# Mode weights in one load of 2 KB runs a tile, in place of two half-partition loads of 4 KB runs

## The chip, the cores and the metric

The kernel runs on one core of one Trainium2 chip. The core has TensorE (PE) for matrix products, VectorE (DVE), ScalarE (ACT), GpSimd (POOL) and SyncE (SP); the last two issue its DMAs, and sixteen DMA engines carry them. The metric is the device time of one execution in microseconds, as a median of several runs. A profiled execution gives the instruction and DMA records.

## The reference

Causal attention over 8 batches, 8 heads, 576 positions and 64 dimensions, with a bias from a running sum of `max(s, 0)`, is followed by a spectral mixing layer. The heads are laid side by side to `x` of shape (8, 576, 512). Cut to what matters here:

```python
X = np.fft.rfft(x, axis=1)                       # 64 modes are used
Xr, Xi = (np.real(X[:, :n_modes]), np.imag(X[:, :n_modes]))
Yr = einsum('bmd,mde->bme', Xr, w_r) - einsum('bmd,mde->bme', Xi, w_i)
Yi = einsum('bmd,mde->bme', Xr, w_i) + einsum('bmd,mde->bme', Xi, w_r)
y = np.fft.irfft(Y, n=S, axis=1)
u = x + y
return u + np.maximum(u @ w_ch, 0.0)
```

`w_r` and `w_i` are 64 x 512 x 512 in float32, 67 MB each. Every element is used once for each of the 8 batches, so nearly all bytes that the kernel reads are these weights.

## The kernel before

The attention runs over 32 steps `n`, each a pair of heads of one batch; 8 steps (the batches) make one of four groups `g`, and a group is a block of 128 channels. A step forms scores, exponentials and the products with `v`, which end in `x_all`. `fft(n)` then takes the 64 Fourier modes of this block by products with a table `Ff_sb` (L427) and copies them from PSUM to `xs` (L437).

`modes(g, c)` multiplies eight modes `8c` to `8c+7` of group `g` with their weights (L449): 16 products of a 32-column block of `xs` with 512 columns of weights, in four column groups of PE, added up in one PSUM tile. The 32 columns of a block belong to two modes, real and imaginary parts and 8 batches.

The weights are read in the order of `wq`: group, chunk `c`, real or imaginary `ri`, and `par`. A tile holds four modes by 128 channels by 512 columns in bfloat16, converted by the DMA from float32, and there are 128 tiles. In the kernel before, `loads_w` fills a tile by two transfers, each of 64 partitions: half `h` takes every second mode, and one partition of it holds two neighbouring channels of a mode, so that 4 KB are read in one run and 2 KB are written in one. The two halves of the partitions belong to different modes, so `xs` has a block for each half and parity of the channel (`q`), with zeros where a mode is not the half's own, and `Ff_np` has its columns sorted by `h`. `fft` therefore runs over two parities, five row blocks and two halves: 20 products of 96 columns and four copies.

The first 8 tiles of weights go to places not in use yet (`early`), the others to rings of 11 and 6 buffers. Which tiles are asked for in which step is planned ahead (`on_chip`, `used`), from how many earlier tiles are used up by then. `load` merges the lists of a step (q, k, v for three steps ahead, and weights) by their positions in them, and issues each transfer on POOL's queue (L224). POOL works through its queue in order; where a buffer is not free or too many transfers are out, it waits, and everything behind it waits too. `load` asks for a single packet request a transfer in both kernels:

```python
nc.gpsimd.dma_start(out=dst, in_=src, single_packet=True)
```

`wch_sb`, the matrix `w_ch`, is loaded once from POOL (L570). SP's queue carries the constants at the start, in each step two rows of the running sum to `qtA` and `qtB` (`cum_rows`, L318 and L319), at the end the row spreads to `yv` (`spread`, L484) and the stores of the result (L766).

After the last step, the eight chunks of the last group remain (from L773): `modes(3, c)`, a transposition and a product with `w_ch` for each, mixed with stored products of `x`. The last chunk's products are mixed with the first sums of the output (`meanwhile`), in another order than in the other calls. Then all pairs of output tiles are finished and stored.

Of the kernel before, what the change touches and what calls it, by code (L numbers as in the profile page):

```python
# [9 lines left out]
FP32 = mybir.dt.float32  # L10
FP16 = mybir.dt.float16
BF16 = mybir.dt.bfloat16
# [6 lines left out]
def kernel(  # L19
# [11 lines left out]
    nc = tc.nc  # L31
    B, H, S, D = q.shape
    NM = moe_w_r.shape[0]
    DM = H * D
    P = 128
    NT = (S + P - 1) // P
    tails = [min(P, S - T * P) for T in range(NT)]
# [8 lines left out]
    MC = 8  # L46
# [7 lines left out]
    W = 2 * P  # L54
    NWN = S // W
    NK = 2 * NWN
    HM = NM // 2
    HP = P // 2


    ident_np = np.eye(P, dtype=np.float32)
# [7 lines left out]
    m_idx = np.arange(NM, dtype=np.float64)  # L69
    ang = 2.0 * np.pi * np.outer(t_idx, m_idx) / S  # L70
    Ff_np = np.zeros((SP, 3 * NM), dtype=np.float16)
    for h in range(2):
        for i, f in enumerate((np.sin(ang), np.cos(ang), -np.sin(ang))):
            Ff_np[:S, (3 * h + i) * HM : (3 * h + i + 1) * HM] = f[:, h::2]
    cmv = np.where(m_idx == 0, 1.0, 2.0) / S
    G_np = np.zeros((NM, 2, SP), dtype=np.float64)
    G_np[:, 0, :S] = cmv[:, None] * np.cos(ang.T)
# [16 lines left out]
    gp = ctx.enter_context(tc.tile_pool(name="globals", bufs=1))  # L94


    x_all = gp.tile([P, NG, B, NT, P], FP16, name="x_all")
    y_acc = gp.tile([P, NCK, DM], FP32, name="y_acc")

    xs = [gp.tile([P, 2, 2, 2, 2, B, HM], BF16, name=f"xs{i}") for i in range(2)]  # L100
    xs_flat = [t.rearrange("p q k h r b m -> p (q k h r b m)") for t in xs]
    ident16h = gp.tile([P, P], FP16, name="ident16h")
    Ff_sb = gp.tile([P, NT, 3 * NM], FP16, name="Ff_sb")
    G_sb = gp.tile([P, SP], FP16, name="G_sb")
# [4 lines left out]
    auxpool = ctx.enter_context(tc.tile_pool(name="aux_psum", bufs=2, space=PSUM))  # L109
# [24 lines left out]
    p_sb = [ap_.tile([P, poff[-1]], FP16, name=f"p_sb{i}") for i in range(NP_)]  # L134
    p4 = [ap_.tile([P, P], FP16, name=f"p4_{i}") for i in range(2)]

    temp = xs_flat[1].bitcast(FP32)
    ident32, negm32, s_sb = temp[:, :P], temp[:, P : P + 2 * W + NL], temp[:NPAIR, -S:]
    ident16 = ap_.tile([P, P], BF16, name="ident16")
    negm = ap_.tile([P, 2 * W + NL], BF16, name="negm")  # L140
# [49 lines left out]
    wt = {}  # L190
# [3 lines left out]
    def ring_of(k):  # L194
        if k < NE:
            return None
        return int(k < LW2 and (k - NE) % (WA + WB) >= WA)

    def loads_w(upto):
        todo = []  # L200
        while len(wt) < min(upto, len(wq)):
            g, c, ri, par = key = wq[len(wt)]
            i = ring_of(len(wt))
            if i is None:
                t = early[len(wt)]
            else:
                t = (wpool, wpool2)[i].tile([P, WM, DM], BF16, name="w_sb", tag="w")
            src = (moe_w_r, moe_w_i)[ri]
            m0 = c * MC + par * MC // 2
            for h in range(2):  # L210
                todo.append((
                    t[HP * h : HP * h + HP].rearrange("p (m q) e -> p m (q e)", q=2),
                    src[m0 + h : m0 + MC // 2 : 2, g * P : (g + 1) * P, :].rearrange(
                        "m (p q) e -> p m (q e)", q=2
                    ),
                ))
            wt[key] = t
        return todo

    def load(*lists):  # L220

        todo = [((i + 0.5) / len(l), x) for l in lists for i, x in enumerate(l)]
        for _, (dst, src) in sorted(todo, key=lambda t: t[0]):
            nc.gpsimd.dma_start(out=dst, in_=src, single_packet=True)  # L224
# [10 lines left out]
    for n in range(N):  # L235
# [3 lines left out]
        while nt < min(w, len(wq)):  # L239
            i = ring_of(nt)  # L240
# [37 lines left out]
    with tc.tile_pool(name="cum_psum", bufs=1, space=PSUM) as cpsum:  # L278
# [5 lines left out]
            out=cum, data0=spos, data1=zer, initial=0.0, op0=ALU.add, op1=ALU.add  # L284
# [16 lines left out]
        for x in range(2):  # L301
            rows = slice(NL * x, NL * x + NL)
            nc.vector.tensor_copy(
                out=cumt4[rows, :], in_=cumt_sb[rows, NK, x::2]
# [8 lines left out]
    def cum_rows(n):  # L313
        if n >= N:
            return
        g, b = divmod(n, B)
        p0 = b * H + 2 * g
        nc.sync.dma_start(out=qtA[n % NQ][D : D + 1, :], in_=ncum_sb[p0 : p0 + 1, :])  # L318
        nc.sync.dma_start(out=qtB[n % NQ][0:1, :], in_=ncum_sb[p0 + 1 : p0 + 2, :])  # L319
# [98 lines left out]
    def fft(n):  # L418
        if n < 0:
            return  # L420
        g, b = divmod(n, B)
        ps = auxpool.tile([P, 2, 3 * HM], FP32, name="ft_ps", tag="aux")
        for q_ in range(2):
            for T in range(NT):
                nT = tails[T]
                for h in range(2):
                    nc.tensor.matmul(  # L427
                        ps[HP * h : HP * h + HP, q_, :],
                        x_all[:nT, g, b, T, q_::2],
                        Ff_sb[:nT, T, 3 * HM * h : 3 * HM * (h + 1)],  # L430
                        start=(T == 0), stop=(T == NT - 1),
                        tile_position=(0, HP * h), skip_group_check=True,
                    )
        for h in range(2):
            rows = slice(HP * h, HP * h + HP)
            for k in range(2):
                nc.vector.tensor_copy(  # L437
                    out=xs[g % 2][rows, :, k, h, :, b, :],
                    in_=ps[rows, :, k * HM : (k + 2) * HM].rearrange("p q (r m) -> p q r m", r=2),
                )  # L440

    def modes(g, c, meanwhile=None):


        ps = auxpool.tile([P, DM], FP32, name="yp", tag="aux")
        cols = xs[g % 2].rearrange("p q k h r b m -> p q k (h r b) m")

        def product(ri, q_, cg):
            nc.tensor.matmul(  # L449
                ps[32 * cg : 32 * cg + 32, :],  # L450
                cols[:, q_, 1 - ri, :, c * MC // 2 + cg],
                wt[(g, c, ri, cg // 2)][:, 2 * (cg % 2) + q_, :],
                start=(ri == 0 and q_ == 0), stop=(ri == 1 and q_ == 1),
                tile_position=(0, 32 * cg), skip_group_check=True,
            )

        for x in range(4):
            ri, y = divmod(x, 2)
            if meanwhile and x in meanwhile:
                meanwhile[x]()  # L460
            for z in range(4):
                if meanwhile:
                    product(ri, z // 2, 2 * y + z % 2)
                else:
                    product(ri, y, z)
        if g == 0:
            nc.vector.tensor_copy(out=y_acc[:, c, :], in_=ps)
        elif g < NG - 1:
            nc.vector.tensor_tensor(out=y_acc[:, c, :], in0=ps, in1=y_acc[:, c, :], op=ALU.add)
        else:  # L470
            yb = spool.tile([P, DM], FP16, name="y_sb", tag="y")
            for cols in halves if c == NCK - 1 else [slice(0, DM)]:
                nc.vector.tensor_tensor(
                    out=yb[:, cols], in0=ps[:, cols], in1=y_acc[:, c, cols], op=ALU.add
                )
            if c >= NCK - 2:
                spread(c, 0, yb)
            return yb
# [3 lines left out]
    def spread(c, which, rows):  # L482

        nc.sync.dma_start(out=yv[16 * c : 16 * c + 16, :, which, :], in_=rows)  # L484
# [53 lines left out]
    with tc.tile_pool(name="sc_psum", bufs=2, space=PSUM) as scpool, \  # L538
            tc.tile_pool(name="tr_psum", bufs=1, space=PSUM) as trpool, \
            tc.tile_pool(name="av_psum", bufs=1, space=PSUM) as avpool:  # L540
        cum_rows(0)
        transposes(0, 0)
        transposes(0, 1)
        load(loads_qkv(2))
        pad_p()
        for n in range(N):
            if n in (0, 2):
                nc.vector.memset(xs_flat[n // 2].bitcast(FP32), 0.0)
            tails_due = loads_tails(n // B + 1)[n % B - 3 : n % B - 2] if 2 < n % B < 5 else []
            load(loads_qkv(n + LA) + tails_due, loads_w(on_chip[n]))  # L550
            cum_rows(n + 1)
            scores(n, 0)
            av(n - 1, 1)
            transposes(n + 1, 0)
            scores(n, 1)
            i = first_pairs[n - N + len(first_pairs)] if n >= N - len(first_pairs) else None
            if i is not None:
                first_transposed(i, 0)
            transposes(n + 1, 1)
            fft(n - 1)  # L560
            av(n, 0)
            if i is not None:
                first_product(i, 0)
                first_transposed(i, 1)
            for c in mode_steps.get(n, []):
                modes(c // NCK, c % NCK)
            if i is not None:
                first_product(i, 1)
            if n == N // 2:
                nc.gpsimd.dma_start(out=wch_sb, in_=moe_w_ch.rearrange("(dt p) e -> p dt e", p=P))  # L570
        av(N - 1, 1)
        fft(N - 1)
    load(loads_w(len(wq)))
    at.close()

# [7 lines left out]
    zpool = ctx.enter_context(tc.tile_pool(name="z_psum", bufs=2, space=PSUM))  # L583

    NLOC = 4
    old = xs_flat[0]
    xt_sb = [
        old[:, i * 2 * DM : (i + 1) * 2 * DM].bitcast(FP16).rearrange("p (x t c) -> p x t c", x=2, c=P)
        for i in range(2)
# [199 lines left out]
    c = NCK - 2  # L789
# [21 lines left out]
    for x in range(2):  # L811
        dts = slice(x * DT // 2, (x + 1) * DT // 2)
        ps = auxpool.tile([P, DT // 2, P], FP16, name="yt_ps", tag="aux")
# [88 lines left out]
```

## Time and profile before

| | |
|---|---|
| median of 3 runs | 453.28 us (452.77 to 454.39) |
| profiled execution: time / span | 452.77 / 451.0 us |
| mean granted clock of PE | 0.879 |
| weight loads of POOL | 256 of 256 KB written (240 to `w_sb`, 16 to early places) |
| q, k, v loads | 32, 32, 72 |
| DMA in all | 93.83 MB, mean 208 GB/s |
| HBM read / written | 164.56 MB / 9.44 MB |

Durations in the profile are those of single instructions; matrix products are pipelined, so that neighbouring ones overlap. The page cuts the span in 40 equal slices of 11.3 us with one digit for the busy tenths. Sizes of DMA packets are those of the bytes written; a weight packet reads twice as many. A line like "L224 POOL" is a DMA's issue and descriptor work on POOL, and not its transfer; transfers are listed with their time from issue to landing. The chain is followed back from the last instruction to what released it.

### The profile page before, as it was taken

The numbers are of one execution on the slowest core, as the hardware profiler recorded it, in microseconds if no ns is written. First come the engines' busy times: TensorE is split into PE (matmuls) and PEld (weight loads), VectorE is DVE, ScalarE is ACT, GpSimd is POOL, SyncE is SP. The second block draws the span as 40 slices with busy tenths as digits, with TensorE's granted clock in tenths as the row PEclk, the third lists the DMA queues.
The fourth block names the chain that finished last, engine by engine and source line by source line (L and its number), as shares of the span: only waits on it lengthen the run. The fifth ranks groups of instructions, "written<-read, shape, count | busy, mean of one in ns | idle before, by whom it ended". The sixth has DMA issues, their size and how long they took to land.

```text
span 451.0 us, 11579 instructions
## 1 busy us (share of the span) xinstructions
PE 359.5 (80%) x4745; PEld 226.5 (50%) x4745; DVE 257.3 (57%) x599; ACT 222.1 (49%) x390; POOL 241.2 (53%) x397
## 2 busy tenths in 40 slices
PE   1789999997566989946777777698897858879995
PEld 1456666665334666624555445456564425534432
DVE  7774776774333576723446545456654643662796
ACT  1584778565333566733435443456550323331774
POOL 7766765765566676455675665566544444420000
PEclk9995999997665699966769989889996986999999
DMA  9999999999999999999999999999999999994688
GB/s 182 200 204 206 204 204 205 205 207 207 207 207 201 196 192 200 208 207 207 204 203 207 208 205 207 207 205 203 207 210 211 209 209 209 210 218 91 236 299 316
DMA packets 77796, 93.83 MB, mean 208 GB/s; under 512 B 30432, under 2 KB 40160, under 8 KB 77744
## 3 DMA queue, kind: packets, MB, share of 16 engines
q0 software_dynamic: 68240, 81.81, 104.8%
q1 hardware_dynamic: 9504, 11.29, 7.9%
q8 instruction: 37, 0.61, 0.5%
q14 instruction: 15, 0.12, 0.1%
HBM read 164.56 MB, written 9.44 MB: 386 GB/s over the span
## 4 chain that ended last, share of the span: by engine, by line
DMA 48%; PE 33%; DVE 9%; issue 5%; POOL 2%; ACT 2%; SPq 0%; DVEq 0%; POOLq 0%; ACTq 0%
DMA w_sb<-in_moe_w_i_dram 21%; DMA w_sb<-in_moe_w_r_dram 14%; DMA q<-in_q_dram 5%; PE av_ps L401 4%; PE sc_ps L372 4%; DMA k<-in_k_dram 3%; PE yp L449 3%; PE ft_ps L427 3%; PE sc_ps L366 3%; PE tr_ps L331 2%; PE z_ps L620 2%; PE z_ps L711 2%; DMA wch_sb<-in_moe_w_ch_dram 2%; DVE qtB L334 2%; PE g_ps L670 2%
## 5 line engine op out<-in xcount | busy, mean ns | idle before, releaser
L380 ACT ACTIVATE p_sb<-sc_ps,cumt_sb 128x576 f16<-128x576 f32 (+1 forms) x256 | 141.9, 635 | 58.7 <-PE sc_ps L372 58.4
L224 POOL DMA_DIRECT2D w_sb<-in_moe_w_r_dram x120 | 71.5, 596 | 60.4 <-DMA w_sb<-in_moe_w_r_dram 20.0
L224 POOL DMA_DIRECT2D w_sb<-in_moe_w_i_dram x120 | 71.5, 597 | 47.6 <-DMA w_sb<-in_moe_w_i_dram 21.5
L224 POOL DMA_DIRECT2D v<-in_v_dram x72 | 51.8, 720 | 22.5 <-DMA w_sb<-in_moe_w_r_dram 7.3
L366 PE MATMUL sc_ps<-negm,ident 128*128 128x256 bf16 x256 | 57.2, 310 | 0.2
L449 PE MATMUL yp<-w_sb,xs 128*32 128x512 bf16 x480 | 37.9, 421 | 12.1 <-DMA w_sb<-in_moe_w_i_dram 7.2
L401 PE MATMUL av_ps<-v,p_sb 128*128 128x65 f16 x1024 | 45.8, 200 | 0.0
L334 DVE COPY ktA<-tr_ps 64x576 bf16<-64x576 bf16 x32 | 24.0, 749 | 37.3 <-PE tr_ps L331 37.3
L331 PE MATMUL tr_ps<-ident,q 64*64 64x64 bf16 x576 | 17.2, 209 | 32.6 <-DMA q<-in_q_dram 32.5
L372 PE MATMUL sc_ps<-qtB,ktB 128*128 128x512 bf16 (+2 forms) x192 | 42.9, 339 | 0.0
L401 PEld LDWEIGHTS <-p_sb 128*128 128x128 f16 x1024 | 40.0, 102 | 5.1 <-DVE x_all L411 1.8
L334 DVE COPY qtA<-tr_ps 64x576 bf16<-64x576 bf16 x32 | 23.8, 743 | 29.6 <-PE tr_ps L331 29.6
L372 PE MATMUL sc_ps<-qtA,ktA 65*128 65x512 bf16 (+2 forms) x192 | 39.2, 316 | 0.4 <-DMA qtA<-ncum_sb 0.4
L406 DVE TENSOR_REDUCE den<-av_ps 128x5 f32<-128x10 f32 x64 | 10.8, 169 | 46.5 <-PE av_ps L401 45.7
L351 ACT ACTIVATE p<-sc_ps,cumt 128x64 f16<-128x64 f32 x32 | 10.0, 313 | 55.0 <-PE sc_ps L347 55.0
L437 DVE CAST xs<-ft_ps 64x128 bf16<-64x128 f32 x128 | 31.4, 284 | 9.4 <-PE ft_ps L427 9.0
L427 PE MATMUL ft_ps<-Ff_sb,x_all 128*64 128x96 f16 (+1 forms) x640 | 34.1, 229 | 1.0 <-DVE x_all L411 1.0
L331 PE MATMUL tr_ps<-ident,k 64*64 64x64 bf16 x576 | 17.2, 208 | 20.2 <-DVE qtB L334 10.2
L411 DVE TENSOR_TENSOR x_all<-av_ps,rcp 128x320 f16<-128x320 f32 x64 | 31.5, 492 | 2.2
L334 ACT COPY ktB<-tr_ps 64x576 bf16<-64x576 bf16 x32 | 20.3, 633 | 23.9 <-DVE ktA L334 22.7
L449 PEld LDWEIGHTS <-xs 128*32 128x32 bf16 x512 | 19.2, 145 | 23.8 <-issue 9.6
L331 PEld LDWEIGHTS <-q 64*64 64x64 bf16 x576 | 13.5, 121 | 35.1 <-DMA q<-in_q_dram 33.9
(117 smaller groups left out, 557.2 us busy)
## 6 DMA issues: line engine op xcount, KB each, us to landing
w_sb<-in_moe_w_r_dram POOLq DMA_DIRECT2D x120, 256.0 KB, 8.0
w_sb<-in_moe_w_i_dram POOLq DMA_DIRECT2D x120, 256.0 KB, 8.1
q<-in_q_dram POOLq DMA_DIRECT2D x32, 144.0 KB, 7.1
k<-in_k_dram POOLq DMA_DIRECT2D x32, 144.0 KB, 7.0
v<-in_v_dram POOLq DMA_DIRECT2D x72, 64.0 KB, 7.1
out_dram<-r_sb SPq DMA_DIRECT2D x16, 256.0 KB, 2.2
out_dram<-r_w SPq DMA_DIRECT2D x16, 256.0 KB, 2.7
x_all<-in_moe_w_i_dram POOLq DMA_DIRECT2D x6, 256.0 KB, 7.2
```

The lines of the kernel that those rows point to most:

```text
L224: nc.gpsimd.dma_start(out=dst, in_=src, single_packet=True)
L331: nc.tensor.transpose(ps[rows, r, :], src[rows, r, :], ident16[rows, rows])
L334: copy(out=dst[n % NQ][rows, :].rearrange("d (p r) -> d p r", r=R), in_=ps[rows].rearrange("d r p -> d p r"),)
L366: nc.tensor.matmul(ps[:, bass.ds(w * S, W)], ident16, negm[:, bass.ts(r, W)], start=True, stop=False, skip_group_check=True,)
L372: nc.tensor.matmul(ps[:, c0 : c0 + i1 - i0], keys[:, w, r, :], qt[:, i0:i1], start=False, stop=True, skip_group_check=True,)
L380: nc.scalar.activation(out=pt[:, poff[x] : poff[x] + S - w * W], in_=ps[:, w * S : (w + 1) * S - w * W], func=ACTF.Exp, bias=cumt_sb[:, x, ...
L401: nc.tensor.matmul(ps[:, I, r : r + NCH], lhsT, rhs, start=(i == 0), stop=(i == len(todo) - 1), skip_group_check=True,)
L406: nc.vector.tensor_reduce(out=den, in_=ps[:, :, 0 : VW : NCH], axis=mybir.AxisListType.X, op=ALU.add)
L411: nc.vector.tensor_tensor(out=x_all[:, g, b, :, D * h : D * h + D], in0=ps[:, :, 1 : NCH], in1=rcp.unsqueeze(2).to_broadcast([P, NT, D]), ...
L427: nc.tensor.matmul(ps[HP * h : HP * h + HP, q_, :], x_all[:nT, g, b, T, q_::2], Ff_sb[:nT, T, 3 * HM * h : 3 * HM * (h + 1)], start=(T == ...
L437: nc.vector.tensor_copy(out=xs[g % 2][rows, :, k, h, :, b, :], in_=ps[rows, :, k * HM : (k + 2) * HM].rearrange("p q (r m) -> p q r m", r=2),)
L449: nc.tensor.matmul(ps[32 * cg : 32 * cg + 32, :], cols[:, q_, 1 - ri, :, c * MC // 2 + cg], wt[(g, c, ri, cg // 2)][:, 2 * (cg % 2) + q_, ...
```

## The change

A weight tile is loaded by one transfer to all 128 partitions, partition `p` holding channel `p` of four modes, in runs of 2 KB read and 1 KB written. `xs` goes back to one block of 64 modes with zeros around it (5,120 elements a partition in place of 4,096), `fft` to five products of 192 columns and two copies, and `modes` to blocks of one mode parity, in the order of the tiles: four products for each of the four tiles. The request for single packets, the order of the tiles, the rings and the plan stay as they are.

```diff
-    for h in range(2):
-        for i, f in enumerate((np.sin(ang), np.cos(ang), -np.sin(ang))):
-            Ff_np[:S, (3 * h + i) * HM : (3 * h + i + 1) * HM] = f[:, h::2]
+    Ff_np[:S, :NM] = np.sin(ang)
+    Ff_np[:S, NM : 2 * NM] = np.cos(ang)
+    Ff_np[:S, 2 * NM :] = -np.sin(ang)
...
-    xs = [gp.tile([P, 2, 2, 2, 2, B, HM], BF16, name=f"xs{i}") for i in range(2)]
+    xs = [gp.tile([P, 5, 2, B, NM], BF16, name=f"xs{i}") for i in range(2)]
...
             src = (moe_w_r, moe_w_i)[ri]
-            m0 = c * MC + par * MC // 2
-            for h in range(2):
-                todo.append((
-                    t[HP * h : HP * h + HP].rearrange("p (m q) e -> p m (q e)", q=2),
-                    src[m0 + h : m0 + MC // 2 : 2, g * P : (g + 1) * P, :].rearrange(
-                        "m (p q) e -> p m (q e)", q=2
-                    ),
-                ))
+            todo.append((
+                t,
+                src[c * MC + par : (c + 1) * MC : 2, g * P : (g + 1) * P, :].rearrange("m p e -> p m e"),
+            ))
...
-        ps = auxpool.tile([P, 2, 3 * HM], FP32, name="ft_ps", tag="aux")
-        for q_ in range(2):
-            for T in range(NT):
-                nT = tails[T]
-                for h in range(2):
-                    nc.tensor.matmul(
-                        ps[HP * h : HP * h + HP, q_, :],
-                        x_all[:nT, g, b, T, q_::2],
-                        Ff_sb[:nT, T, 3 * HM * h : 3 * HM * (h + 1)],
...
+        ps = auxpool.tile([P, 3 * NM], FP32, name="ft_ps", tag="aux")
+        for T in range(NT):
+            nT = tails[T]
+            nc.tensor.matmul(
+                ps,
+                x_all[:nT, g, b, T, :],
+                Ff_sb[:nT, T, :],
+                start=(T == 0), stop=(T == NT - 1),
+            )
+        for ri in range(2):
+            nc.vector.tensor_copy(
+                out=xs[g % 2][:, 3 - 2 * ri, :, b, :],
+                in_=ps[:, (1 - ri) * NM : (3 - ri) * NM].rearrange("p (r m) -> p r m", r=2),
+            )
...
         for x in range(4):
-            ri, y = divmod(x, 2)
+            ri, par = divmod(x, 2)
+            cols = xs[g % 2].rearrange("p k r b m -> p (k r b) m")
+            c0 = (48, 16)[ri] - 16 * par
...
-            for z in range(4):
-                if meanwhile:
-                    product(ri, z // 2, 2 * y + z % 2)
-                else:
-                    product(ri, y, z)
+            for cg in range(4):
+                nc.tensor.matmul(
+                    ps[32 * cg : 32 * cg + 32, :],
+                    cols[:, c0 : c0 + 32, c * MC + 2 * cg + par],
+                    wt[(g, c, ri, par)][:, cg, :],
```

The clears of `xs` (L548), the views of it that hold constants at the start and `xt_sb` at the end follow its new form.

More of the change, by code (lines that the diff above doesn't have):

```diff
@@ L56 @@
     NK = 2 * NWN
-    HM = NM // 2
-    HP = P // 2
     ident_np = np.eye(P, dtype=np.float32)
@@ L98 @@
     y_acc = gp.tile([P, NCK, DM], FP32, name="y_acc")
-    xs = [gp.tile([P, 2, 2, 2, 2, B, HM], BF16, name=f"xs{i}") for i in range(2)]
-    xs_flat = [t.rearrange("p q k h r b m -> p (q k h r b m)") for t in xs]
+    xs = [gp.tile([P, 5, 2, B, NM], BF16, name=f"xs{i}") for i in range(2)]
     ident16h = gp.tile([P, P], FP16, name="ident16h")
@@ L135 @@
     p4 = [ap_.tile([P, P], FP16, name=f"p4_{i}") for i in range(2)]
-    temp = xs_flat[1].bitcast(FP32)
+    temp = xs[1].rearrange("p k r b m -> p (k r b m)").bitcast(FP32)
     ident32, negm32, s_sb = temp[:, :P], temp[:, P : P + 2 * W + NL], temp[:NPAIR, -S:]
@@ L421, in fft @@
         g, b = divmod(n, B)
-        ps = auxpool.tile([P, 2, 3 * HM], FP32, name="ft_ps", tag="aux")
-        for q_ in range(2):
-            for T in range(NT):
-                nT = tails[T]
-                for h in range(2):
-                    nc.tensor.matmul(
-                        ps[HP * h : HP * h + HP, q_, :],
-                        x_all[:nT, g, b, T, q_::2],
-                        Ff_sb[:nT, T, 3 * HM * h : 3 * HM * (h + 1)],
-                        start=(T == 0), stop=(T == NT - 1),
-                        tile_position=(0, HP * h), skip_group_check=True,
-                    )
@@ L434, in fft @@
[L434 to L440, printed above, removed]
+        ps = auxpool.tile([P, 3 * NM], FP32, name="ft_ps", tag="aux")
[7 more added lines that the diff above has]
+            )
@@ L442, in modes @@
+        for ri in range(2):
[3 more added lines that the diff above has]
+            )
     def modes(g, c, meanwhile=None):
         ps = auxpool.tile([P, DM], FP32, name="yp", tag="aux")
[L446 to L455, printed above, removed]
@@ L457, in modes @@
         for x in range(4):
-            ri, y = divmod(x, 2)
+            ri, par = divmod(x, 2)
+            cols = xs[g % 2].rearrange("p k r b m -> p (k r b) m")
+            c0 = (48, 16)[ri] - 16 * par
             if meanwhile and x in meanwhile:
                 meanwhile[x]()
-            for z in range(4):
-                if meanwhile:
-                    product(ri, z // 2, 2 * y + z % 2)
-                else:
-                    product(ri, y, z)
+            for cg in range(4):
[3 more added lines that the diff above has]
+                    wt[(g, c, ri, par)][:, cg, :],
+                    start=(x == 0), stop=(x == 3),
+                    tile_position=(0, 32 * cg), skip_group_check=True,
+                )
@@ L547 @@
             if n in (0, 2):
-                nc.vector.memset(xs_flat[n // 2].bitcast(FP32), 0.0)
+                nc.vector.memset(xs[n // 2].rearrange("p k r b m -> p (k r b m)").bitcast(FP32), 0.0)
             tails_due = loads_tails(n // B + 1)[n % B - 3 : n % B - 2] if 2 < n % B < 5 else []
@@ L585 @@
     NLOC = 4
-    old = xs_flat[0]
+    old = xs[0].rearrange("p k r b m -> p (k r b m)")
     xt_sb = [
```

## The prediction

> **What bounds the kernel now.** I read the page first, for the shares of the engines and of the DMA.
>
> ```profile
> PE 359.5 (80%) x4745; PEld 226.5 (50%) x4745; DVE 257.3 (57%) x599; ACT 222.1 (49%) x390; POOL 241.2 (53%) x397
> ...
> DMA  9999999999999999999999999999999999994688
> ...
> q0 software_dynamic: 68240, 81.81, 104.8%
> ```
>
> The reader is to see that no compute engine is full, while the DMA row is at 9 for 36 of 40 slices. Queue q0, which carries every load issued by GpSimd, has packet time for 104.8% of sixteen engines' span although it stops about 40 us before the end, so its packets overlap. Then I asked who waits (POOL's line and PE's), and looked at POOL's timeline near the end of the loads.
>
> ```profile
> POOL w_sb L224 <- DMA w_sb<-in_moe_w_i_dram: 38.9, 60, 1.8
> ...
> PE tr_ps L331 <- DMA q<-in_q_dram: 34.5, 11, 5.9
> ```
>
> ```profile
> 372.86 0.59 POOL L224 DMA_DIRECT2D w_sb<-in_moe_w_r_dram  x1 [0.47 <-DMA w_sb<-in_moe_w_r_dram]
> ...
> 382.88 0.59 POOL L224 DMA_DIRECT2D w_sb<-in_moe_w_r_dram  x1 [0.47 <-DMA w_sb<-in_moe_w_r_dram]
> ...
> 392.90 0.59 POOL L224 DMA_DIRECT2D w_sb<-in_moe_w_r_dram  x1 [0.47 <-DMA w_sb<-in_moe_w_r_dram]
> ```
>
> Between these lines stand eight loads of 256 KB each: 10.02 us for eight, 1.253 us for one half-tile. POOL issues in 0.59 us and then waits for a landing, some eight loads back (8 x 1.25 us is the 9.7 us to landing of this stretch). So the queue is never empty, and the weights' rate is that of the DMA engines. Last, the chain in order of time, at the place where loads hand over to compute:
>
> ```profile
> 360.06 9.96 DMA w_sb<-in_moe_w_i_dram
> 370.01 0.04 issue
> 370.06 1.09 PE yp L449 x5
> 371.14 0.02 issue
> 371.17 0.70 DVE y_sb L473
> ```
>
> At 370.06 the products of chunk 3 of the last group (tiles 109 to 112 of 128) have waited for the last of their tiles; from there the chain is compute to the end, 81 us. So the end is set by the landing of tile 112 plus a fixed rest, as long as the last 16 tiles are not later still. Their slack: the last weight packet ends at 411.1, and its products start at 412.38 (the chain's last "PE yp L449 x4"), about 1.2 us later.
>
> **The price of a packet.** The DMA records of the trace have start, size and duration of every packet. Taking distances between the starts of packets that follow each other on one engine: 2,048 bytes written, the weights now, every 154.0 ns (duration 173); 1,152 bytes, q and k, every 88.3; 1,024 bytes every 78.8 (duration 98); 256 bytes, v, every 22.4; the 4-byte completion write takes 21. The distances lie on one line, 3.4 ns a packet and 0.0736 ns a byte. Together: 8 x 154.0 + 21 = 1,253 ns, the pace above. The 1,024-byte row is `wch_sb`, whose load (float32 to a 2-byte type, rows of 2 KB, 128 partitions x 4 rows, the same single-packet request) has the form that a weight tile gets:
>
> ```profile
> wch_sb<-in_moe_w_ch_dram POOLq DMA_DIRECT2D x1, 512.0 KB, 7.8
> ```
>
> **The change part by part, against the profiled execution (452.77 us, its span 451.0 and 1.77 around it; the median of the three runs, 453.28, is 0.51 above it).**
>
> *The loads.* A tile is now two transfers, each 8 packets of 2,048 bytes and a completion per engine: 2 x 1,253 = 2,506 ns. It becomes one of 32 packets of 1,024 bytes and one completion: 32 x 78.8 + 21 = 2,543 ns. That is 36.5 ns more a tile, from 16 more packets at 3.4 less one completion at 21. Up to tile 112 it is 4.1 us, and up to the last, 4.7 us, all of it on the path. Bounds: were the 3.4 ns hidden, 2,434 ns a tile, 8 us less at tile 112; were nothing overlapped, 98 ns a packet, 3,157 ns a tile, 73 us more. Both are far from the row that has the very form, so I take its 78.8; an error of 0.5 ns in it is 16 ns a tile, 1.8 us.
>
> *POOL's issues.* 256 weight issues of 0.597 us (153 us) go, and 128 come. Nearest row: `wch_sb` 0.74, so 95 us. POOL then waits for landings instead; 58 us of busy time off the path. If it cost more, up to 2.5 us each would still be covered by the transfer itself.
>
> *The queue.* The wait that stops POOL is counted in transfers, about eight. Eight of the new ones are twice the bytes, so the queue is deeper. What that can give: by the packet prices, the engines are mostly 98 to 100% filled from 10 to 400 us, the unfilled part adding to 4.6 us. The clearest hole is at 163 to 166 us, 0.67 us, after POOL issued nothing between 161.09 and 163.45. Bounds are 0 and 4.6; I take 0.6, that hole alone, because the rest is spread evenly over the span, about as much as the small transfers of q1 take (some 1% of the engines).
>
> *The transforms.* 640 matmuls of L427 (25.4 + 15.5 us busy) become 160 of 192 columns; 20 now take 0.97 us of PE an iteration, 5 perhaps half of that. 128 copies of L437 at 284 ns become 64 with as many elements a partition: DVE 18 us less. The two clears of L548, 1.77 us each, grow by a quarter, 0.9 us together. All of this is hidden by the loads for q and weights, which PE waits for after 100 us; before that a faster PE gets ahead of a full queue. Were the cover gone, PE would gain some 0.5 us an iteration. I count zero.
>
> *The order of the products.* Now 6 of 16 products wait for the last tile of a chunk (two before the step of y, four after); after it, 4. At 370.06 six took 1.07 us and four elsewhere take 0.65: 0.4 less.
>
> *Small transfers on SP's queue.* On each engine a weight packet request is 1.25 us now and 2.54 then, and an SP transfer has to get between them. The rows of `qtA` land in 4.9 us among loads, against 2.2 to 2.9 for stores when no load is queued: about two packet requests. So I expect about 7.4. They are sent 10 us before use (56.70 for a score at 66.8), so this is hidden. The row spread of chunk 5 (`yv<-v_sb`, issued by 400.1, 6.9 at most) lands by about 407 and is read at 410.5; 2.5 us more is still inside.
>
> Sum: +4.1 - 0.6 - 0.4 = +3.1 us: 455.9 on the profiled execution, 456.4 on the median. The last tile confirms it: 4.7 - 0.6 later less 1.2 of slack is +2.9, so the two ends come within 0.2 us of each other.
>
> The Trainium skill, "DMA: Bandwidth & Descriptors", section "Anatomy of one DMA — SWDGE (gpsimd) path", gives a fit of about 2.0 us fixed plus bytes over 436 GB/s for each transfer, and its "Rules for kernel authors" advise one 128-partition transfer over two on disjoint halves. By that fixed cost, paid in sequence, 128 transfers fewer would save 256 us. The trace has 1.253 us for a whole half-tile with eight in flight and 21 ns for its completion, so the fit would put this kernel at an impossible 200 us and I do not use it. The section "Why small descriptors are slow (HBM only)" of the same page speaks against the change: a fixed few cycles for each packet. The 3.4 ns of the rows is of that sort.
>
> **The rivals.**
>
> *Absorbed.* The deeper queue and the shorter PE iterations close half of the unfilled 4.6 us and more: +4.1 - 0.4 - 2.9 = +0.8, 454.1. For: the stretch 147 to 166 has several slow slices. Against: from 370 to 400 us the engines are filled to 99.6%, and that with weight tiles alone.
>
> *Not slower.* The deeper queue closes all of it: 4.1 - 0.4 - 4.6 = -0.9, 452.4. The place is 20 to 370 us; it decides from 3.7 us of gaps closed on. Against: the small transfers of q1 use part of that time themselves.
>
> *The small transfers become a wait.* A spread has several packets per engine, each behind 2.54 us. With two more such waits for `yv<-v_sb` of chunk 5 it lands at 412 in place of 407 and the first products with `yv` (410.5) stand still for 1.5 to 2 us behind it, PE's queue with them: 458.2. It decides from 3.5 us of extra landing time on.
>
> *The price of the row is too low.* One 512 KB load is little evidence; were it 80.5 ns in steady state, 54 ns a tile come on top, 6 us: 462.
>
> **How the numbers follow.** Forecast 0.62; absorbed 0.13; not slower 0.07; small transfers 0.12; dearer packets 0.06. The measurement tells about 0.3%, 1.4 us, from no change. The forecast's own range is 455.0 to 457.8 (0.5 ns on the packet, 0 to 1.8 us of gaps). The whole range leaves out the dearest case and most of the not-slower one: 453.4 to 459.2. Slower: the forecast, small transfers and dearer packets, 0.80; same: absorbed and a part of not slower, 0.15; faster 0.05.
>
> **What would show it.** Weights at one transfer of 512 KB every 2.54 us in the last stretch; 1,024-byte packets at 78.8 ns; about 128 issues near 0.74 us; the hand-over after chunk 3 at 373.2 in place of 370.06; `qtA` landing near 7.4 us. The prediction is wrong if the pace is under 2.50 or over 2.58 us, or if the last chain no longer has a weight landing near 370 us.

## The result, and the profile after

The changed kernel takes 455.81 us (median of 4 runs, 455.45 to 456.52) against 453.38 (4 runs, 452.77 to 454.39) in the same comparison. The ratio is 1.0053, with a 95% interval of 1.0031 to 1.0075. That is 2.4 us slower; 3.1 was forecast. The profiled execution took 455.45 us, its span is 453.7.

The page of the changed kernel: busy time of the engines, the DMA row in 40 slices, and the queue of POOL's loads with packets, MB and share of sixteen engines' span.

```profile
PE 344.1 (76%) x4265; PEld 219.0 (48%) x4265; DVE 240.4 (53%) x535; ACT 222.2 (49%) x390; POOL 182.9 (40%) x269
...
DMA  9999999999999999999999999999999999995688
...
q0 software_dynamic: 98960, 81.81, 113.8%
```

All three engines that the change relieves have less to do: POOL 58 us, DVE 17 us, PE 15 us. The bytes of q0 are the same, in 30,720 more packets. The DMA row stays full. Its digits say little by themselves, since packets overlap (113.8% in q0); holes are counted below from the prices of the packets.

POOL's timeline in the last stretch of weights (start, duration, instruction, idle time before it and what ended it):

```profile
365.60 0.74 POOL L217 DMA_DIRECT2D w_sb<-in_moe_w_r_dram  x1 [1.76 <-DMA w_sb<-in_moe_w_r_dram]
368.14 0.74 POOL L217 DMA_DIRECT2D w_sb<-in_moe_w_r_dram  x1 [1.80 <-DMA w_sb<-in_moe_w_r_dram]
370.75 0.74 POOL L217 DMA_DIRECT2D w_sb<-in_moe_w_i_dram  x1 [1.86 <-PE yp L441]
...
391.49 0.74 POOL L217 DMA_DIRECT2D w_sb<-in_moe_w_i_dram  x1 [9.83 <-PE yp L441]
```

A whole tile now goes every 2.5 us. In the DMA records the completions of one tile and the next on one engine are 2,542 to 2,543 ns apart, where two half-tiles took 2,506. POOL is no longer stopped by landings alone, as its waits show (total us, times, longest):

```profile
POOL w_sb L217 <- PE yp L441: 50.9, 18, 9.8
POOL w_sb L217 <- DMA w_sb<-in_moe_w_r_dram: 31.1, 19, 2.5
```

The longest wait, 9.83 us up to 391.49, is now for a buffer that the products still use. Enough loads are out to cover it: by the prices of the packets the engines stand unfilled for less than 0.1 us between 381 and 392.

The chain in order of time, at the hand-over from loads to compute:

```profile
352.93 19.81 DMA w_sb<-in_moe_w_i_dram
372.78 0.69 PE yp L441 x4
373.49 0.70 DVE y_sb L455
```

The last tile of chunk 3 releases four products at 372.78, where six started at 370.06. From there to the end it is compute in this profile, 81 us as before.

### The profile page after: what moved, and what is told of

The parts are those of the page before. It is cut to its first block, busy times and chain, and to the rows that moved or that the text cites. A ratio compares the mean times of both kernels' runs of the same rounds, so it can differ in the third digit from the quotient of the medians.

```text
span 453.7 us, 10402 instructions
## 1 busy us (share of the span) xinstructions
PE 344.1 (76%) x4265; PEld 219.0 (48%) x4265; DVE 240.4 (53%) x535; ACT 222.2 (49%) x390; POOL 182.9 (40%) x269
## 3 DMA queue, kind: packets, MB, share of 16 engines
q0 software_dynamic: 98960, 81.81, 113.8%
## 4 chain that ended last, share of the span: by engine, by line
DMA 51%; PE 29%; DVE 8%; issue 7%; POOL 3%; ACT 2%; SPq 0%; DVEq 0%; POOLq 0%; ACTq 0%
DMA w_sb<-in_moe_w_i_dram 19%; DMA w_sb<-in_moe_w_r_dram 14%; DMA q<-in_q_dram 13%; PE sc_ps L365 4%; PE av_ps L394 3%; PE sc_ps L359 3%; PE tr_ps L324 2%; POOL w_sb L217 2%; DMA k<-in_k_dram 2%; PE z_ps L602 2%; PE yp L441 2%; PE z_ps L693 2%; PE g_ps L652 2%; PE u_ps L712 2%; PE u_ps L693 1%
## 5 line engine op out<-in xcount | busy, mean ns | idle before, releaser
L217 POOL DMA_DIRECT2D w_sb<-in_moe_w_i_dram x60 | 45.0, 751 | 86.0 <-PE yp L441 42.8
L217 POOL DMA_DIRECT2D w_sb<-in_moe_w_r_dram x60 | 45.4, 757 | 62.7 <-DMA w_sb<-in_moe_w_r_dram 27.1
L217 POOL DMA_DIRECT2D v<-in_v_dram x72 | 50.7, 706 | 30.5 <-DMA v<-in_v_dram 8.6
L441 PE MATMUL yp<-w_sb,xs 128*32 128x512 bf16 x480 | 36.0, 405 | 16.1 <-DMA w_sb<-in_moe_w_i_dram 12.7
L365 PE MATMUL sc_ps<-qtB,ktB 128*128 128x512 bf16 (+2 forms) x192 | 45.7, 357 | 0.0
L365 PE MATMUL sc_ps<-qtA,ktA 65*128 65x512 bf16 (+2 forms) x192 | 37.3, 304 | 0.4 <-DMA qtA<-ncum_sb 0.4
L441 PEld LDWEIGHTS <-xs 128*32 128x32 bf16 x512 | 22.4, 170 | 25.5 <-issue 21.5
L365 PEld LDWEIGHTS <-ktB 128*128 128x128 bf16 x192 | 23.1, 120 | 16.0 <-issue 7.4
L217 POOL DMA_DIRECT2D k<-in_k_dram x32 | 17.6, 551 | 20.4 <-DMA w_sb<-in_moe_w_r_dram 7.4
```

What stands on the lines that cost most here:

```text
L365: nc.tensor.matmul(ps[:, c0 : c0 + i1 - i0], keys[:, w, r, :], qt[:, i0:i1], start=False, stop=True, skip_group_check=True,)
L441: nc.tensor.matmul(ps[32 * cg : 32 * cg + 32, :], cols[:, c0 : c0 + 32, c * MC + 2 * cg + par], wt[(g, c, ri, par)][:, cg, :], start=(x == ...
```

## The experiments

Times are medians. There are three series, each with its own runs of the kernel before on the same chip: 453.26 us (17 runs; e1, e3, e4 and e7), 453.98 (11; e8 to e11) and 453.65 (13; e5 and e6).

Unfilled time means here: from the first packet of POOL's queue to the last packet of tile 112, less the time of that queue's packets by their prices, as a mean of the sixteen engines. That last packet is found by its place in the order of starts over all engines. Each figure comes from one profile, and two profiles of one kernel differed by up to 1.4 us.

**Twice the completions.** Two transfers of 64 partitions a tile, in 2 KB runs:

```diff
-            todo.append((t, src[...].rearrange("m p e -> p m e")))
+            for h in range(2):
+                r0 = P // 2 * h
+                todo.append((
+                    t[r0 : r0 + P // 2],
+                    src[c * MC + par : (c + 1) * MC : 2, g * P + r0 : g * P + r0 + P // 2, :].rearrange(
+                        "m p e -> p m e"
+                    ),
+                ))
```

> The changed kernel, each weight tile loaded by two transfers of 64 partitions again, but in 2 KB runs: the packets stay at 1,024 bytes written, the completions double, and eight transfers out hold half the bytes. Theory (price of packets, and a deeper queue that fills holes): a tile costs 2 x (16 x 78.8 + 21) = 2,564 ns in place of 2,543, +2.4 us at tile 112, and the 1.6 us that the changed kernel gained in unfilled time (7.86 us before, 6.22 after, up to tile 112) come back: 455.8 + 4.0 = 459.8. Rival, holes filled by the shorter steps and not by the queue: +2.4 alone, 458.2. Rival, the time goes by bytes alone: 455.8.

Measured: 459.56 us, ratio 1.0130 [1.0107, 1.0153]. The records have a completion every 1,281 ns, 2,562 a tile: the price is as worked out. Unfilled time is 8.15 us, 1.9 more than in the first profile of the changed kernel. The price of 2.4 and this 1.9 make 4.3, the difference of the two profiled executions (459.76 and 455.45). Bytes alone (455.8) are ruled out; the price alone (458.2) is 1.4 us below the measured time, and this rival is taken up again in the table of four. The chain of this kernel shows one thing that was not expected:

```profile
394.73 9.96 DMA w_sb<-in_moe_w_i_dram
404.98 12.20 DMA w_sb<-in_moe_w_i_dram
417.22 0.47 PE yp L445 x2
417.69 0.54 PE z_ps L697 x2
...
419.56 0.48 PE yp L445 x4
```

It stays on the loads up to tile 127, whose products start at 417.22. The semaphore events of the trace have the landing of tile 128 complete at 419.52, 0.04 us before its products. In the kernel before this slack was 0.44 us (411.94 to 412.38), in the changed kernel 0.43 (414.77 to 415.20): here it is used up.

**Twice the packets.** Each row of a tile is cut in two runs of 1 KB, each transfer holding half the columns of four modes; the products read the two halves of a row through one access pattern.

```diff
+            tv = t.rearrange("p m e -> p (m e)").rearrange("p (y m e) -> p y m e", y=2, m=WM)
+            for y in range(2):
+                todo.append((
+                    tv[:, y],
+                    src[
+                        c * MC + par : (c + 1) * MC : 2, g * P : (g + 1) * P, bass.ts(y, DM // 2)
+                    ].rearrange("m p e -> p m e"),
+                ))
...
-                    wt[(g, c, ri, par)][:, cg, :],
+                    wt[(g, c, ri, par)].rearrange("p m e -> p (m e)").rearrange(
+                        "p (y m e) -> p y m e", y=2, m=WM
+                    )[:, :, cg],
```

> The changed kernel, each weight tile loaded by two transfers of half the columns, so that runs are 1 KB read and 512 bytes written: twice the packets of the changed kernel, four times those of before. Theory (3.4 ns a packet and 0.0736 ns a byte): 2 x (32 x 41.1 + 21) = 2,672 ns a tile, 130 ns more than the changed kernel, 14.5 us at tile 112 and 16.6 at the last, which has 0.8 us of slack: 455.8 + 15.8 = 471.6, the last tiles now setting the end. Rival, only completions cost: 455.8 + 2.4 = 458.2. Rival, the time goes by bytes alone: 455.8.

Measured: 475.59 us, ratio 1.0487 [1.0460, 1.0514]. Both rivals fall. Packets of 512 bytes follow every 41.1 ns and a tile takes 2,675 ns, 3 from the line. The total is 4 us over the expectation, and that is no price: unfilled time up to tile 112 is 11.4 us, 5 more than in the changed kernel, in the first 20 us and around 140 to 180, 240 and 320 us. Landings set the pace to the end:

```profile
424.77 11.71 DMA w_sb<-in_moe_w_i_dram
436.52 0.48 PE yp L445 x4
437.02 0.43 DVE y_sb L461
```

**The transform's work given back.** The changed kernel, but each half of the 192 columns formed twice, and copies of 64 partitions:

```diff
+        for again in range(2):
+            for y in range(2):
+                cs = slice(y * 3 * NM // 2, (y + 1) * 3 * NM // 2)
+                for T in range(NT):
+                    nT = tails[T]
+                    nc.tensor.matmul(ps[:, cs], x_all[:nT, g, b, T, :], Ff_sb[:nT, T, cs], ...)
```

> The changed kernel with the transform's work of before: 20 products of 96 columns (each half of the columns formed twice) and four copies of 64 partitions in a step, weights as in the changed kernel. Theory (the shorter steps count nothing, the queue hides them): 455.8 within 0.7, unfilled time up to tile 112 still near 6.2 us. Rival (the shorter steps are what filled the holes): the 1.6 us come back, 457.4, unfilled time near 7.9 us.

Measured: 456.99 us, ratio 1.0074 [1.0053, 1.0096], between the two. Its profile was its slowest run (457.92), with 8.3 us unfilled. And the edit gives back more than was taken: its products fill 128 columns of PE where those of before fill 64, so that the copies wait 30.3 us for them between 20 and 330 us (7.7 before) and PE is busy for 373.0 us (359.5 before). So I ran a table of four on one chip.

> The changed kernel itself, as the first cell of a table of four on one chip: one or two transfers a tile, short or long transforms. Expected 455.8 within 0.5, with about 0.3 us of unfilled time from 140 to 180 us as in its first profile (1.8 in the kernel before).

> Second cell: one transfer a tile, the transform's work of before. The first time it was 457.0, between the 455.8 of one reading (the shorter steps count nothing) and the 457.4 of the other (they fill the holes). If the shorter steps count, it is 0.8 to 1.6 us over the changed kernel in the same call; if not, within 0.4 of it.

> Third cell: two transfers of half the partitions a tile, short transforms. The price of 16 x 2 packets and two completions gives 2.4 us over the changed kernel. If the queue's depth counts too, it is 3.2 to 4.0 over it (the first time 3.8 by the medians); if not, 2.0 to 2.8.

> Fourth cell: two transfers a tile and the transform's work of before; against the kernel before only the runs are shorter (2 KB, not 4 KB). If depth and shorter steps each fill a part, both losses add to the price of 2.4: 2.4 + 1.4 + 1.2 = 5.0 over the changed kernel, 460.8. If they fill the same hole and one without the other is enough to lose it, it equals the third cell, about 459.6.

The fourth is both edits at once. Measured, us, in brackets over the first cell; then unfilled time up to tile 112 and its part from 140 to 180 us:

| | short transforms | long transforms |
|---|---|---|
| one transfer a tile | 456.07; 6.8; 0.4 | 456.95 (+0.9); 6.9; 0.4 |
| two transfers a tile | 459.04 (+3.0); 8.2; 1.0 | 459.15 (+3.1); 7.7; 1.0 |

The kernel before in the same series: 453.98, so the changed kernel's ratio is 1.0048 [1.0031, 1.0065] here. Two transfers a tile cost 3.0 with the short transforms and 2.2 with the long ones, where 2.4 is their price. What is left, +0.6 and -0.2, is within the interval, so the times don't show what the queue's depth is worth. The hole at 140 to 180 goes with the number of transfers, with either transform. The long transforms cost 0.9 in the upper row and 0.1 in the lower; as they are longer than those of before, 0.9 bounds what the shorter ones gave. This 0.9 isn't time unfilled up to tile 112, which differs by 0.1 in the upper row. In that cell's profile the landing of tile 128 sets the end, as the landings of tiles 127 and 128 do in the two profiles of the lower row:

```profile
397.37 18.99 DMA w_sb<-in_moe_w_i_dram
416.40 0.47 PE yp L446 x4
```

Why it lands later there was not settled.

**Half the completions, with 4 KB runs.** The kernel before, with the two tiles of a real or imaginary part in one buffer and one transfer of four modes for each half of the partitions. The first stretch of tiles uses the early places in pairs; chunks 3 and 7 of the last group keep single tiles for the imaginary part, and the plan of what is asked for in which step is made in pairs.

```diff
-    WA, WB = 11, 6
+    WA, WB = 6, 3
...
-                t = (wpool, wpool2)[i].tile([P, WM, DM], BF16, name="w_sb", tag="w")
+                d = (wpool, wpool2)[i].tile([P, 2 * WM, DM], BF16, name="w_sb", tag="w")
...
+            parts_ = [(t, c * MC + par * MC // 2, MC // 2) for par, t in enumerate(ts)]
+            if d is not None and not (g == NG - 1 and ri == 1 and c in (3, NCK - 1)):
+                parts_ = [(d, c * MC, MC)]
+            for t, m0, nm in parts_:
+                for h in range(2):
+                    todo.append((
+                        t[HP * h : HP * h + HP].rearrange("p (m q) e -> p m (q e)", q=2),
+                        src[m0 + h : m0 + nm : 2, g * P : (g + 1) * P, :].rearrange(
+                            "m (p q) e -> p m (q e)", q=2
+                        ),
+                    ))
```

> The kernel before with its 4 KB runs, but the two tiles of a real or imaginary part taken together: each half of the partitions is loaded by one transfer of four modes, 512 KB, into one buffer of two tiles (rings of 6 and 3 such buffers in place of 11 and 6). Packets stay at 2,048 bytes, completions halve, eight transfers out hold twice the bytes. Theory: 42 ns less for each of 54 pairs up to tile 112, 2.3 us, and the 1.6 us of holes that a deeper queue fills: 453.4 - 3.9 = 449.5. Rival (the queue's depth gives nothing): 451.1. Rival (buffers of two tiles come free later, POOL is stopped, new holes): 453.4 or more.

Measured: 451.68 us (12 runs), ratio 0.9963 [0.9944, 0.9983]: faster than both kernels, by 1.6 us against the one before. The price is as worked out, a completion every 2,486 ns and 2.3 us less packet time up to tile 112. The fill is not: 9.9 us unfilled in a profile that was its slowest run (453.65), 0.4 more than before in the first 20 us, 1.0 from 20 to 60 and 0.2 from 140 to 180. So no gain of a deeper queue shows here: of the 2.3 us, 1.6 arrive. POOL's waits name buffers of two tiles as well as landings:

```profile
POOL w_sb L233 <- DMA w_sb<-in_moe_w_r_dram: 43.2, 23, 2.5
POOL w_sb L233 <- DMA w_sb<-in_moe_w_i_dram: 37.2, 25, 2.2
POOL w_sb L233 <- PE yp L458: 17.7, 3, 8.4
```

Whether the coarser buffers, the coarser plan or the coarser mixing with q, k and v made these holes was not separated.

**Without the single-packet request.** `single_packet=True` is left out of `load` in the changed kernel and in the kernel before.

> The changed kernel without the single-packet request on POOL's loads. In the changed kernel SP's rows of qtA land in 4.6 us beside loads whose packet requests last 2.54 us on an engine, where 7.4 was predicted. Theory: an SP transfer does not wait for the end of a load's request, so the request's length is not what sets its landing; without the request qtA lands in 4.5 to 4.9 us again, packets of 1,024 bytes stay at 78.8 ns and the time at 455.8 to 456.1. Rival: the request is what lets packets overlap; without it they follow at their duration, 98 ns, 3,157 ns a tile, some 70 us more.

> The kernel before without the single-packet request. Theory: 2,048-byte packets at 154.0 ns as before, qtA at 4.6 to 4.9 us, 453.4 to 454.0. Rival: packets follow at their duration, 173 ns, 2,810 ns a tile, 34 us more. The difference of the two kernels without the request tells whether the gain of long runs hangs on it.

Measured: 455.89 us, ratio 1.0056 [1.0041, 1.0071], and 453.54, ratio 0.9996 [0.9981, 1.0012]. The distances stay at 78.8 and 154 ns, the rows of `qtA` land in 4.6 and 5.0 us. The request makes no difference that shows in either layout, and the difference of the two layouts does not hang on it. The packet counts are the same too, so the runs don't tell whether the request changes anything in what is sent.

## Why the prediction was right

**The price of a packet: right, and the largest term.** From the packets in the records, work up to the last packet of tile 112 is 357.53 us a DMA engine before and 361.63 after: 4.10 more, where 4.1 was predicted from a single 512 KB load of the same form. The pace was 2,543 ns to the digit. The kernel with 512-byte packets and the pair kernel follow the same line, from 512 to 2,048 bytes.

**The hand-over: right in place.** It was put at 373.2 and came at 372.78, still behind tile 112. By the prediction's own terms it belonged at 373.6, as the 0.4 us of the products comes after it; the queue's larger term made the difference.

**The last tile: its slack misread.** The prediction took 1.2 us, from the end of the last packet to the products. But products wait for the landing, which came at 411.94, so the slack was 0.44. With this the sum through the last tile would have been 4.7 - 0.6 - 0.4 = 3.7 and not 2.9, and the last tile, not the hand-over, would have set the end. In the profiled execution it didn't: more holes were filled than the 0.6 taken, so that the last landing came only 2.8 us later, and the path through the hand-over was as late by then. It is close: in the profile of the changed kernel without the request, the chain stays on the loads up to tile 127.

**The order of the products: right for the profiled executions.** At the hand-over, 1.09 us of products became 0.69, as the two chains show. In both the granted clock was 0.50 there. In two profiles in which it was still 1.00, six products took 0.70 us (the kernel before without the request) and four 0.48 (the changed kernel again), so that the term is then 0.2.

**The queue: right in sign, its term too small, and the hole that was named closed for another reason.** I took 0.6 us of holes filled. Unfilled time up to tile 112 fell from 7.86 us to 6.22 in one profile and 6.77 in another: 1.1 to 1.6. (Both sides include 3.1 to 3.3 us of the first 20 us, when the queue fills; the prediction's 4.6 counted from 10 us.) Without the request it was 8.9 and 7.2. The rivals "absorbed" and "not slower" needed 2.9 and 4.6 us. What was filled lies mostly between 140 and 180 us, in two holes (unfilled us):

| | 140 to 160 | 160 to 180 |
|---|---|---|
| before: two transfers a tile, 4 KB runs | 0.8 | 1.0 |
| changed: one transfer, 2 KB runs | 0.1 | 0.2 to 0.3 |
| two transfers, 2 KB runs (three profiles) | 0.8 to 0.9 | 0.2 to 0.3 |
| one transfer, 2 KB runs, long transforms (two profiles) | 0.15 and 0.45 | 0.3 |
| two transfers, 1 KB runs | 1.4 | 0.7 |
| pairs: 512 KB transfers, 4 KB runs | 0.8 | 1.2 |

The first hole goes with the number of transfers a tile, as a deeper queue would have it, but the pair kernel has it too, with transfers as large. The second is the one that the prediction named, behind this gap of POOL:

```profile
163.45 0.60 POOL L224 DMA_DIRECT2D w_sb<-in_moe_w_r_dram  x1 [2.37 <-issue]
```

It is as small with two transfers of 2 KB runs a tile, whose queue holds no more bytes than before, and stays with the pairs. So the deeper queue isn't what closed it. It goes with the 2 KB runs and the order of products that comes with them, with short or long transforms; which of these, and why, was not settled. That a hole of about the same size (0.7 us) closed with the number of transfers was luck. The prediction counted the shorter transforms at zero because the loads hide them; the table of four puts them at 0.9 us or less.

**The fixed rest: 0.4 us off.** From the step after the products to the end it was 79.8 us before and 80.2 after. In both profiles the granted clock is at 0.50 for 10.24 us around this place, from 369.2 to 379.4 before and from 372.8 to 383.1 after. Counted from the hand-over it thus lasts 9.4 us and 10.3 us, and the stretch that follows the hand-over by 8 to 16 us ran at another mean clock (the last number columns are clock, DMA share and GB/s); first the kernel before, then the changed one:

```profile
379.00:387.00 8.00, 7.01 (x63) 5.13 (x63) 5.13 (x8) 3.79 (x7) 3.71 (x7) 0.97 1.12 209
```

```profile
381.50:389.50 8.00, 7.01 (x59) 5.06 (x57) 4.66 (x8) 3.62 (x7) 0.15 (x1) 0.90 1.24 207
```

The chains have the same products in it, again first before, then after:

```profile
379.01 0.77 PE xt_ps L610 x8
379.77 1.73 PE z_ps L620 x8
```

```profile
381.33 0.97 PE xt_ps L592 x8
382.30 2.17 PE z_ps L602 x8
```

They take 0.64 us more, of which some comes back later.

The sum of the profile is thus 4.1 - 1.6 - 0.4 + 0.4 = 2.5, against 2.7 of span; the last 0.2 is the spread of the engines. The work is a mean of sixteen, but a tile has landed when the last of them is done: the sixteen completions of its last transfer arrive over 3.0 us before and 3.8 after, so that the products start 2.0 and 2.2 us behind the packet that is last by the count. So the 2.7 of span against the forecast 3.1 is partly compensation, and to that extent luck: the queue gave up to 1.0 more than was taken, and the clock and the spread, which no term had, took 0.6 back.

**Small transfers on SP's queue: wrong.** The prediction took the 4.9 us of `qtA` among loads as two packet requests of 1.25 us on top of 2.2 to 2.9, and expected 7.4. DMA issues, first of the kernel before, then of the changed one (last column: median us to landing):

```profile
qtA<-ncum_sb SPq DMA_DIRECT2D x32, 1.1 KB, 4.9
```

```profile
qtA<-ncum_sb SPq DMA_DIRECT2D x32, 1.1 KB, 4.6
```

With requests twice as long it is even shorter. In the records the first 72-byte packet starts 3.8 us after the start of the issue, before and after the change (medians 3.80 and 3.85), and the rest follow within 0.6 and 0.3 us. So the length of a load's request is not what the small transfer waits for, and the rival built on it had no ground. It cost the forecast nothing, since the term was zero; the chance of 0.12 on that rival was misplaced.

**POOL and DVE: right, and hidden as said.** 0.75 us an issue where 0.74 was taken; the two clears take 2.19 us each, 0.85 more together, where 0.9 was.

## What to carry to other kernels

Where the DMA row is full from end to end, price a change of layout by the distance between the starts of packets on one engine, not by their duration: here 3.4 ns a packet, 0.0736 ns a byte written and 21 ns a completion, with which the four other layouts that were run came out within 3 ns a tile. Then find the landing that hands over to compute, and the slack of the landings behind it, taken from the landing and not from the last packet, before multiplying by the number of tiles. Longer runs and fewer, larger transfers both pay by that sum, but they also change what POOL waits for, and the holes that this opened or closed here, 1 to 2 us, were about as large as the gain.

## What the runs showed of the hardware that was not expected

- The single-packet request on POOL's loads changed nothing that can be measured: 455.89 us without it in one layout, 453.54 in the other, with the same packet distances.
- An SP transfer of 16 packets among loads had its first packet 3.8 us after the start of its issue (medians of four profiles, 3.80 to 3.85), whether a load's packets on an engine lasted 1.25 or 2.54 us, with the request or without it.
- The duration of a packet in the records (173 ns for 2,048 bytes, 98 for 1,024) is about 19 ns longer than the distance to the next on its engine, so a queue's share of time can pass 100%.
- The sixteen engines are not in step: the sixteen completions of the transfer that ends tile 112 arrived over 3.0 us in the kernel before and 3.8 us in the changed one, and the products waited for the last.
